# A fused attention and feed-forward kernel: all weight casts on VectorE, nine landing slots, eight float32 steps in the second product

## The chip, the cores and the metric

The kernel runs on one core of one Trainium2 chip. The metric is the device time of one execution in microseconds; the kernel before has a median of 746.74 us over three runs (746.36 to 748.03).

## The reference

Eight batches of 576 rows pass through an attention over 32 memory slots per head (8 heads of 64), and the result through a feed-forward block with weights of 512 x 2048 and 2048 x 512:

```python
a = softmax(phi over the 32 memory slots)             # per batch, head, row
k_m = einsum('bhsm,bhsd->bhmd', a, k)                 # 32 x 64 per head
v_m = einsum('bhsm,bhsd->bhmd', a, v)
attn = softmax((q @ k_m^T) / sqrt(64))                # 576 x 32 per head
x = concatenate over heads of (attn @ v_m)            # 4608 x 512
h = x @ w_in                                          # 4608 x 2048
g = h * erf(softplus(h))
out = g @ w_out                                       # 4608 x 512
```

## The kernel before, in words

**Tiling.** The work goes through 128 steps. A step is one batch b of 8 and one block k of 16, where a block is 128 of the 2048 hidden columns (`ORDER`, L273). The kernel never forms x: per batch it multiplies v_m into w_in on TensorE (`vw`, L624), and the *first product* (`ffn1`, L698, matmuls at L711) multiplies the attention weights by that, giving 128 hidden columns by 576 rows in two halves of 288. A copy out of PSUM gives h (L726, L727), ScalarE makes softplus and erf of it (L734, L739) in groups of steps (`GROUPS`, L274: four groups of 4, then groups of 6), since the two functions need different tables. `g_split` (L742) multiplies by h. The *second product* (`ffn2`, L799, matmuls at L795) adds g times w_out into four PSUM tiles of 128 rows; the last 64 rows of each batch (the "rest") go through DRAM (`rest_d`) and are taken for two batches together (`ffn2_rest`, L819).

**Two precisions of matmul.** Most products are made from values split in a rounded half and a remainder in the type fp32r: three matmuls (rounded by rounded, and the two mixed ones) stand for one. To split costs a ScalarE instruction (L362) and a VectorE one (L364) for weights and attention, and a VectorE cast (L765) and subtraction (L766) for g. The first steps work without a split, in plain float32, each matmul as two instructions: steps below `FR1` in the first product, steps below `FR2` in the second. `FR2` is 4. For these steps g is multiplied into its tile by L749 alone, and GpSimd splits only the rest's 64 columns (L759, L760), which SP then stores (L770). The block's chunk of w_out is used as decoded (`raw_of`) and is split later for the following batches: `split_wo` of chunk c is put at step `second[2c] - 2`, or, for a chunk that float32 steps use, at `second[16 + 2c] - 5`.

**The weights' way in.** Each of the 16 chunks (8 of w_in, called in0 to in7, and 8 of w_out, out0 to out7) is 1 MB. `load_weight` (L382) takes a slot of the pool `wo`, clears the slot's last 16-bit column with a memset on GpSimd (L385) and loads the rest by a DMA on SP (L387). The load lies one 16-bit piece off, and `decode` (L413) puts the numbers together again: a cast of the top pieces (on VectorE, L447, or on GpSimd, L448), a scaling of the low pieces (ScalarE, L449, or VectorE, L451), and a merge on VectorE (L442). A chunk of w_in is merged into a tile `wi`, which has two slots of two chunks each, and this tile is stored to DRAM (`w_in_d`, L457) for the later batches; its landing slot is then free. A chunk of w_out is merged in place.

**The slots.** The pool `wo` has `WB = NPR + 2`, that is 10, slots (NPR is 8). In this order it holds the first two tiles of q, the 16 chunks, and the split chunks of w_out (L465). A tile gets a slot only when every earlier one has one. So the split tiles come after all loads, and each split frees the slot of the chunk that it was made from.

**The order.** `Plan.order` (L125) is a list scheduler that runs when the kernel is built. Each operation has an engine or several ways (`other`), a cost in ns and a rank (100 times the step at which it is wanted). The scheduler keeps clocks for the engines and for landings, counts slots, takes for an operation with several ways the one that ends first (`best_way`, L150), and writes each engine's queue in the resulting order. On the chip every engine runs its queue in that order and waits where an input is late. The cast has the cost 1330 on VectorE and 2300 on GpSimd, a memset 100 on GpSimd, a load's issue 60 on SP. A memset and the load into the same tile wait for one another in the order in which the scheduler happened to write them.

Of the kernel before, what the change touches and what calls it, by code (L numbers as in the profile page):

```python
# [29 lines left out]
PE, DVE, ACT, POOL, SP = "PE", "DVE", "ACT", "POOL", "SP"  # L30
# [38 lines left out]
class Plan:  # L69
# [21 lines left out]
    def op(self, engine, cost, rank, reads, writes, emit, kind=None, nbytes=0, edge=None, after=(),  # L91
           holds=(), other=()):
        x = Op({engine: (cost, emit), **dict(other)}, rank, kind, nbytes, edge)
        x.before.update(after)
        for w, keys in ((False, reads), (True, writes)):
            for k in keys:
                k, part = (k[0], k[1]) if isinstance(k[0], tuple) else (k, None)
                x.tiles.add(k)
                for q, (wrote, read) in self.seen.setdefault(k, {}).items():
                    if q == part or q is None or part is None:  # L100
                        x.before.update(wrote)
                        if w:
                            x.before.update(read)
        for w, keys in ((False, reads), (True, writes)):
            for k in keys:
                k, part = (k[0], k[1]) if isinstance(k[0], tuple) else (k, None)
                s = self.seen[k]
                if w and part is None:
                    s.clear()
                wrote, read = s.setdefault(part, ([], []))  # L110
                if w:
                    wrote[:] = [x]
                    read.clear()
                else:
                    read.append(x)
        x.before.discard(x)
        for k in x.tiles:
            if k in self.users:
                self.users[k].append(x)
                x.placed.append(k)  # L120
        x.placed += [k for k in holds if k not in x.tiles]
        self.ops.append(x)
        return x
# [113 lines left out]
def tile_memory_attention_then_erf_softplus_ffn(  # L237
# [11 lines left out]
    nc = tc.nc  # L249
# [11 lines left out]
    NPR = DFF // 256  # L261
# [6 lines left out]
    assert NC == -(-S // ROW) and D < ROWS[-1]  # L268
    RAW = 5
    HB, EB, GB = 8, 7, 3  # L270
    WB = NPR + 2
    SCALE = 1.0 / float(D) ** 0.5
    ORDER = [(b, k) for b in range(B) for k in range(NK)]  # L273
    GROUPS = [4] * 4 + [6] * 18 + [2, 2]  # L274
    LAG = 8
    assert sum(GROUPS) == NS
    FR1, FR2 = 4, 4
    H_EITHER = 16

    pools = {  # L280
# [1 line left out]
        for n, b, kw in (  # L282
            ("const", 1, {}),
            ("wo", WB, {}),
            ("wi", 2, {}),
# [12 lines left out]
    const = pools["const"]  # L298
    room = {"wo": WB, "wi": 2, "vw_hi": 2, "vw_lo": 2, "at_hi": 4, "at_lo": 4, "h": HB, "e": EB}
    room.update({"g": GB, "rx": 2, "rr": 2, "raw": RAW, "ps": 4, "sc": 2, "dk": 1, "phiT": 2})  # L300
# [22 lines left out]
    def tile_(tag, *key, shape=None, dtype=F32, pool=None):  # L323
        key = plan.tile(tag, *key)
        p, s, d = SHAPES.get(tag, (pool, shape, dtype))
        T[key] = lambda: pools[p].tile(s, d, name=key[0], tag=tag, bufs=BUFS.get(tag))
        return key

    def get(key):
        if callable(T[key]):  # L330
            T[key] = T[key]()
        return T[key]
# [5 lines left out]
    def on_dve(n, inputs=2):  # L338
        return n / 0.96 + 85 if inputs == 2 else n / 1.92 + 75
# [73 lines left out]
    def decode(rank, name, c):  # L413
        key, n = ("w", name, c), 2 * DM
        dst = key
        if name == "in":
            w = ("wi", 0, c // 2)
            if c % 2 == 0:
                tile_("wi", *w)
            dst = (w, c % 2)  # L420

        def pieces():
            v = get(key).bitcast(U32).rearrange("p (n two) -> p n two", two=2)
            return v[:, :, 0], v[:, :, 1]

        def to():
            if name == "in":
                return get(w)[:, :, c % 2 * 256 : (c % 2 + 1) * 256]
            wf[c] = get(key).bitcast(F32)[:, :n].rearrange("p (j d) -> p j d", d=DM)
            return wf[c].rearrange("p j d -> p (j d)")  # L430

        def top(f):
            def emit():
                v = get(key).rearrange("p (n four) -> p n four", four=4)[:, :, 2]
                f(v.bitcast(F16), v.bitcast(BF16))
            return emit

        def merge():
            low, v = pieces()
            if name == "in":  # L440
                low, v = (x.rearrange("p (r f) -> p r f", r=NP_) for x in (low, v))
            nc.vector.scalar_tensor_tensor(  # L442
                out=to().bitcast(U32), in0=v, scalar=16, in1=low,
                op0=ALU.logical_shift_left, op1=ALU.bitwise_or)

        op(DVE, 1330, rank, [(key, "top")], [(key, "top")],
           top(lambda y, x: nc.vector.tensor_copy(out=y, in_=x)),  # L447
           other={POOL: (2300, top(lambda y, x: nc.gpsimd.tensor_copy(out=y, in_=x)))})  # L448
        op(ACT, 1330, rank, [(key, "low")], [(key, "low")], lambda: nc.scalar.activation(  # L449
            pieces()[0].bitcast(I32), pieces()[0], AF.Identity, scale=LOW),  # L450
           other={DVE: (on_dve(n, 1), lambda: nc.vector.tensor_scalar_mul(  # L451
               out=pieces()[0].bitcast(I32), in0=pieces()[0], scalar1=LOW))})
        op(DVE, on_dve(n), rank, [key], [dst], merge)
        if name == "out":
            raw_of[c] = dst
        elif c % 2:
            op(SP, 60, rank, [w], [("w_in", c // 2)], lambda: nc.sync.dma_start(  # L457
                out=w_in_d[c // 2], in_=get(w)), nbytes=P * 8192)
# [404 lines left out]
    for n, name in enumerate(FIRST):  # L863
        x, rank = int(name[-1]) if name[-1].isdigit() else 0, n - 2000
# [12 lines left out]

    memories(at(-10), at(-9), 0, EARLY)
    decode(at(-3), "in", 0)
    for u in range(2):  # L880
        attention(at(-8), at(-7 + 2 * u), u)
# [7 lines left out]
    for c in range(NPR):  # L889
        if c:  # L890
            when(2 * c - 3, decode, at(2 * c - 3), "in", c)
            when(2 * c - 1, vw, at(2 * c - 1.5), 0, c, 1, 2 * c < FR1)
        when(2 * c, decode, at(second[2 * c] - 2.5), "out", c)
        n = second[16 + 2 * c] - 5 if 2 * c < FR2 else second[2 * c] - 2
        when(n, split_wo, at(n), c)
# [105 lines left out]
```

## Time and profile before

| | us |
|---|---|
| median of three runs | 746.74 |
| the profiled execution | 746.22 |
| its span in the trace | 743.6 |
| PE (TensorE) busy | 711.6 |
| DVE (VectorE) busy | 516.7 |
| ACT (ScalarE) busy | 387.7 |
| POOL (GpSimd) busy | 44.2 |

Nine casts of chunks run on VectorE (13.7 us together) and seven on GpSimd (20.5 us). In a group's row, the first part names line, engine, operation and tiles, "x" the count; behind the bar stand the busy time, the mean ns of one, the idle time of the engine just before these instructions, and what ended it. In a timeline each row is a start, a length and an operation, with the idle time in front of it in brackets. PE is TensorE's matmuls and PEld its weight loads. The granted clock is the share of full speed that TensorE was given.

### The profile page before, as it was taken

To read this page: it belongs to the slowest core of one execution; us is meant where nothing else is said; L and a number is where in the kernel's file an instruction comes from. 1 tells how busy PE (TensorE), PEld (TensorE's weight loads), DVE (VectorE), ACT (ScalarE), POOL (GpSimd) and SP (SyncE) were. 2 spreads that over 40 slices of the span, in tenths; PEclk is the share of its full clock that TensorE was granted. 3 is DMA by queue.
4 is the path that set the end of the run, shared out by engine and by line. 5 is a ranking of instruction groups with operands and counts; after the bars stand their busy time and mean duration, and the time that the engine had idled before them with its cause. 6 is when DMAs were issued, how large, how long until landed. Compare 5 with 4: busy or idle time off the path is not lost.

```text
span 743.6 us, 12315 instructions
## 1 busy us (share of the span) xinstructions
PE 711.6 (96%) x4899; PEld 566.3 (76%) x4899; DVE 516.7 (69%) x956; ACT 387.7 (52%) x603; POOL 44.2 (6%) x69
## 2 busy tenths in 40 slices
PE   8866699999999999999999999999999999999997
PEld 3442377887888888888888878888888878888886
DVE  3664999989945597786963867687675567865730
ACT  3642677855942457366381638436454272653701
POOL 0014420000000000000000000000000000002230
PEclk9988799999999999999999999999999999999999
DMA  9996496556362353626262456335241343201002
GB/s 337 417 378 225 126 323 217 207 195 199 111 226 72 127 182 122 225 68 218 77 224 92 160 170 235 106 110 188 68 145 58 123 127 89 86 22 58 1 0 71
DMA packets 66666, 114.96 MB, mean 155 GB/s; under 512 B 37553, under 2 KB 45745, under 8 KB 62513
## 3 DMA queue, kind: packets, MB, share of 16 engines
q1 hardware_dynamic: 66608, 114.18, 45.0%
q8 instruction: 38, 0.62, 0.3%
q14 instruction: 20, 0.16, 0.1%
HBM read 93.19 MB, written 20.97 MB: 154 GB/s over the span
## 4 chain that ended last, share of the span: by engine, by line
PE 82%; DMA 12%; DVE 5%; issue 0%; ACT 0%; SPq 0%; POOL 0%; POOLq 0%; DVEq 0%; ACTq 0%
PE pso L795 44%; PE psh L711 24%; PE psr L795 6%; DMA w<-w_in 6%; PE psa L613 5%; DMA kv<-kv 3%; PE psa L561 2%; DMA phiT<-phiT 1%; DMA out<-ot 1%; DVE w L442 1%; DVE w L447 1%; DVE wi L442 1%; PE psa L583 0%; DVE pmx L477 0%; DVE e L749 0%
## 5 line engine op out<-in xcount | busy, mean ns | idle before, releaser
L795 PE MATMUL pso<-wo,g 128*128 128x512 f32 x1488 | 369.0, 394 | 0.5 <-DVE g L766 0.5
L795 PEld LDWEIGHTS pso<-wo,g 128*128 128x128 f32 x1488 | 270.7, 188 | 61.8 <-issue 9.7
L734 ACT ACTIVATE e<-h 128x576 f32<-128x576 f32 x128 | 86.1, 683 | 209.0 <-DVE h L726 208.5
L726 DVE COPY h<-psh 128x288 f32<-128x288 f32 x240 | 106.8, 451 | 27.6 <-PE psh L711 26.4
L765 DVE CAST g<-e 128x576 fp32r<-128x576 f32 x124 | 56.2, 454 | 86.1 <-PE pso L795 76.7
L711 PE MATMUL psh<-at_hi,vw_hi 128*128 128x288 f32 x496 | 111.2, 306 | 4.6 <-DVE vw_lo L364 4.5
L711 PEld LDWEIGHTS psh<-at_hi,vw_hi 128*128 128x128 f32 x496 | 85.8, 192 | 32.0 <-DVE vw_lo L364 6.5
L711 PE MATMUL psh<-at_lo,vw_hi 128*128 128x288 f32 x496 | 107.7, 299 | 0.0
L711 PE MATMUL psh<-at_hi,vw_lo 128*128 128x288 f32 x496 | 107.3, 298 | 0.0
L749 DVE TENSOR_TENSOR e<-e,h 128x576 f32<-128x576 f32 x124 | 90.8, 750 | 14.6 <-ACT e L739 14.6
L766 DVE TENSOR_TENSOR g<-e,g 128x576 fp32r<-128x576 f32 x124 | 93.2, 752 | 1.7
L711 PEld LDWEIGHTS psh<-at_hi,vw_lo 128*128 128x128 f32 x496 | 81.3, 192 | 0.0
L711 PEld LDWEIGHTS psh<-at_lo,vw_hi 128*128 128x128 f32 x496 | 80.7, 191 | 0.0
L739 ACT ACTIVATE e<-e 128x576 f32<-128x576 f32 x128 | 80.3, 676 | 0.3
L362 ACT ACTIVATE vw_hi<-psa 128x512 fp32r<-128x512 f32 (+1 forms) x68 | 35.2, 554 | 46.1 <-PE psa L613 45.9
L775 POOL CAST rr<-g 128x64 fp32r<-128x64 f32 x32 | 17.8, 566 | 610.0 <-DVE g L765 604.8
L364 DVE TENSOR_TENSOR vw_lo<-psa,vw_hi 128x512 fp32r<-128x512 f32 (+1 forms) x68 | 41.9, 634 | 11.8 <-ACT vw_hi L362 11.7
L795 PE MATMUL psr<-wo,rr 128*128 128x512 f32 x192 | 49.1, 392 | 0.0
L795 PEld LDWEIGHTS psr<-wo,rr 128*128 128x128 f32 x192 | 36.1, 188 | 7.9
L613 PE MATMUL psa<-wi,vm 64*32 64x512 f32 (+1 forms) x576 | 37.9, 566 | 3.9 <-DVE vw_lo L364 2.2
L842 ACT ACTIVATE ot<-pso 128x512 f32<-128x512 f32 x32 | 18.6, 592 | 41.6 <-PE pso L795 35.5
L734 ACT ACT_TABLE_LOAD x24 | 30.8, 1283 | 2.3 <-DVE h L726 1.9
(73 smaller groups left out, 499.4 us busy)
## 6 DMA issues: line engine op xcount, KB each, us to landing
wi<-w_in_d SPq DMA_DIRECT2D x28, 1024.0 KB, 5.3
kv<-kv SPq DMA_DIRECT2D x32, 640.0 KB, 8.2
q<-qT SPq DMA_DIRECT2D x16, 576.0 KB, 6.1
out<-ot SPq DMA_DIRECT2D x32, 256.0 KB, 2.1
w<-w_in SPq DMA_DIRECT2D x8, 1023.8 KB, 16.5
w<-w_out SPq DMA_DIRECT2D x8, 1023.8 KB, 11.6
rr<-rest_d SPq DMA_DIRECT2D x28, 256.0 KB, 2.9
rest_d<-g SPq DMA_DIRECT2D x108, 64.0 KB, 2.1
```

The lines of the kernel that those rows point to most:

```text
L362: lambda: nc.scalar.activation(get_hi(), get_src(), AF.Identity))
L364: lambda: nc.vector.tensor_tensor(out=get_lo(), in0=get_src(), in1=get_hi().bitcast(F32), op=ALU.subtract))
L613: nc.tensor.matmul(out=get(ps[par])[p * M : (p + 1) * M, :], lhsT=w()[rows, p, :], rhs=x()[rows, p, :], start=True, stop=True,)
L711: nc.tensor.matmul(out=get(ps), lhsT=x[:, g, k % 4 * P : (k % 4 + 1) * P], rhs=y[:, g, :], start=(n + g == 0), stop=(n == len(parts) - 1 a ...
L726: lambda: nc.vector.tensor_copy(out=keep(), in_=get(ps)),
L734: last[:] = [op(ACT, on_act(S), rank, [("h", i)], [e], lambda: nc.scalar.activation(get(e), get(("h", i)), AF.Softplus), kind="softplus", ...
L739: last[:] = [op(ACT, on_act(S), rank, [e], [e], lambda: nc.scalar.activation(get(e), get(e), AF.Erf), kind="erf", edge=edge, after=last)]
L749: op(DVE, on_dve(S), rank, [e, h], [to if i >= FR2 else (t, 0)], lambda: nc.vector.tensor_tensor(out=get(t)[:, 0].bitcast(F32) if i < FR2 ...
L765: op(DVE, on_dve(S, 1), rank, [e], [(t, 0)], lambda: nc.vector.tensor_copy(out=get(t)[:, 0], in_=get(e)))
L766: op(DVE, on_dve(S), rank, [e, (t, 0)], [(t, 1)], lambda: nc.vector.tensor_tensor(out=get(t)[:, 1], in0=get(e), in1=get(t)[:, 0].bitcast(F ...
L795: nc.tensor.matmul(out=o, lhsT=y, rhs=z, start=(start and n == 0), stop=(stop and n == len(parts) - 1))
L842: lambda: nc.scalar.activation(get(t)[:, :DM], get(o), AF.Identity))
```

## The change

Three things: the cast of a chunk's top pieces has only VectorE as its way; the pool `wo` has 9 slots instead of 10; and the second product uses float32 for steps 0 to 7 instead of 0 to 3. By the rule above the splits of chunks 2 and 3 of w_out thus move from steps 8 and 10 to steps 23 and 25.

```diff
-    WB = NPR + 2
+    WB = NPR + 1
...
-    FR1, FR2 = 4, 4
+    FR1, FR2 = 4, 8
...
         op(DVE, 1330, rank, [(key, "top")], [(key, "top")],
-           top(lambda y, x: nc.vector.tensor_copy(out=y, in_=x)),
-           other={POOL: (2300, top(lambda y, x: nc.gpsimd.tensor_copy(out=y, in_=x)))})
+           top(lambda y, x: nc.vector.tensor_copy(out=y, in_=x)))
```

## The prediction

> **What bounds the kernel now.** I read the page first, for where TensorE is not full.
>
> ```profile
> span 743.6 us, 12315 instructions
> PE   8866699999999999999999999999999999999997
> ```
>
> The profiled execution took 746.2 us: this span and 2.6 us around it. The median shown is 746.7, half a microsecond more. One digit is the busy tenths of 18.6 us. TensorE is short in the first five slices and full from the sixth on. So I split the span by hand, at the points where TensorE's filling changes (columns: length, busy us and instructions of PE, PEld, DVE, ACT and POOL, granted clock, DMA share, GB/s).
>
> ```profile
> 32.00:42.00 10.00, 5.14 (x20) 3.38 (x19) 2.26 (x4) 4.11 (x8) 2.79 (x7) 0.99 0.99 386
> 42.00:61.00 19.00, 17.21 (x80) 11.74 (x80) 9.86 (x18) 9.25 (x15) 0.00 (x0) 0.82 0.84 326
> 61.00:103.00 42.00, 26.93 (x196) 16.65 (x196) 36.98 (x44) 23.54 (x39) 22.63 (x19) 0.76 0.67 222
> 103.00:200.00 97.00, 96.47 (x735) 77.23 (x737) 90.07 (x171) 73.38 (x113) 0.00 (x0) 1.00 0.56 193
> ```
>
> From 103 to 200 us TensorE lacks 0.5 us of 97, and the page's row stays at 9 to the last slice. What it gets done earlier before 103 brings the end forward, and whatever matmul time is added makes the end later. Between 32 and 103 us it lacks 4.9 + 1.8 + 15.1 = 21.8 us, and at the granted clocks of 0.82 and 0.76 another 17.21 x 0.18 + 26.93 x 0.24 = 9.6 us: 31 us are the most that any change of this stretch could win. Next, the waits from 30 to 110 us (total, times, longest).
>
> ```profile
> PE pso L795 <- issue: 8.2, 2, 6.9
> PE psh L711 <- DVE vw_lo L364: 4.5, 1, 4.5
> PE psa L490 <- ACT bias L484: 4.3, 2, 3.9
> DVE w L442 <- POOL w L448: 18.3, 2, 10.5
> POOL w L385 <- DMA w<-w_in: 55.8, 5, 26.1
> ```
>
> VectorE waited twice, 18.3 us in all, at the merge of a chunk (L442) for its cast on GpSimd (L448). The timelines of GpSimd and VectorE say why (start, length, operation, and in brackets the idle time in front).
>
> ```profile
> 35.01 0.10 POOL L385 MEMSET w<- 128x1 uint16 x1 [2.41 <-DMA w<-w_out]
> 37.55 0.20 POOL L385 MEMSET w<- 128x1 uint16 x4 [2.44 <-DMA w<-w_in]
> 37.69 2.45 POOL L448 CAST w<-w 128x1024 f16<-128x1024 bf16 x1
> 61.05 0.14 POOL L385 MEMSET w<- 128x1 uint16 x2 [20.92 <-DMA w<-w_in]
> 61.13 4.72 POOL L448 CAST w<-w 128x1024 f16<-128x1024 bf16 x2
> 71.43 6.95 POOL L448 CAST w<-w 128x1024 f16<-128x1024 bf16 x2
> 91.35 2.89 POOL L448 CAST w<-w 128x1024 f16<-128x1024 bf16 x1 [0.63 <-DMA w<-w_out]
> 95.89 3.46 POOL L448 CAST w<-w 128x1024 f16<-128x1024 bf16 x1 [1.65 <-DMA w<-w_out]
> ...
> 40.17 1.23 DVE L442 SCALAR_TENSOR_TENSOR w<-w 128x1024 uint32<-128x1024 uint32 x1 [7.74 <-POOL w L448]
> 63.61 3.08 DVE L442 SCALAR_TENSOR_TENSOR w<-w 128x1024 uint32<-128x1024 uint32 x1 [10.51 <-POOL w L448]
> 72.85 3.21 DVE L447 CAST w<-w 128x1024 f16<-128x1024 bf16 x1
> 77.37 1.84 DVE L442 SCALAR_TENSOR_TENSOR w<-w 128x1024 uint32<-128x1024 uint32 x1
> 92.00 3.07 DVE L442 SCALAR_TENSOR_TENSOR w<-w 128x1024 uint32<-128x1024 uint32 x1
> 97.17 3.02 DVE L442 SCALAR_TENSOR_TENSOR wi<-w 128x1024 uint32<-128x1024 uint32 x1
> ```
>
> GpSimd runs its queue in order. Its casts stand behind one-column memsets (L385) that wait for a landing, until 37.5 and again for 20.9 us until 61.0. The chunks to be cast had landed before: the merges at 40.17 and 63.61 are of out0 and out1 (I place them by the order of the chunks), and out1's own memset is one of those released before 35. So the 7.7 and the 10.5 us are waits for a place in a queue, not for data. TensorE's 4.5 us wait (for a vw_lo, queued on VectorE behind the first merge) and its 6.9 us wait (second product of step 2, which reads out1) are their images.
>
> **Part by part: the casts.** Durations as least/median/greatest, and the groups of the operations that the longer float32 stretch drops and adds (busy us, mean ns):
>
> ```profile
> L448 POOL CAST w<-w x7: 2449/2894/3677, 37.7 to 95.9; 128x1024 f16<-128x1024 bf16 x7
> L447 DVE CAST w<-w x9: 1261/1314/3205, 14.5 to 95.7; 128x1024 f16<-128x1024 bf16 x9
> L765 DVE CAST g<-e 128x576 fp32r<-128x576 f32 x124 | 56.2, 454 | 86.1 <-PE pso L795 76.7 <-DMA rest_d<-g 7.9 <-POOL rr L775 1.0
> L766 DVE TENSOR_TENSOR g<-e,g 128x576 fp32r<-128x576 f32 x124 | 93.2, 752 | 1.7
> L364 DVE TENSOR_TENSOR wo<-w,wo 128x1024 fp32r<-128x1024 f32 x8 | 9.7, 1208 | 0.0
> L759 POOL CAST rx<-g 128x64 fp32r<-128x64 f32 x4 | 2.1, 526 | 0.0
> L760 POOL TENSOR_TENSOR rx<-g,rx 128x64 fp32r<-128x64 f32 x4 | 2.4, 599 | 0.3
> ```
>
> Seven casts move to VectorE: 7 x 1.31 = +9.2 us there. The five long VectorE rows above all lie beside a cast on GpSimd; against 1.23 for a merge and 1.31 for a cast they lose 1.85 + 1.90 + 0.61 + 1.84 + 1.79 = 8.0 us, which goes. With the seven casts gone, the two waits of 18.3 us go as such. What replaces them on VectorE is a cast that waits for its own landing, and behind it in VectorE's queue the copies of h (L726) and vw_lo, for which TensorE waits. For out0 and out1 this is nothing; for the later chunks it is the second rival.
>
> **Eight float32 steps.** Steps 4 to 7 lose their rounding (L765) and remainder (L766) on VectorE: 4 x (0.454 + 0.752) = -4.8 us. The splits of out2 and out3 (2 x 1.21 us on VectorE) leave the stretch for steps 23 and 25, where VectorE is 93% busy and TensorE full; I cost them there at nothing, 2.4 us at most if VectorE falls behind. On TensorE a step of the second product is eight float32 instructions instead of twelve:
>
> ```profile
> 57.33 3.60 PE L795 MATMUL pso<-w,g 128*128 128x512 f32 x8
> 67.83 6.01 PE L795 MATMUL pso<-w,g 128*128 128x512 f32 x8 [6.91 <-issue]
> 103.40 5.76 PE L795 MATMUL pso<-wo,g 128*128 128x512 f32 x24
> 43.10 0.68 PE L711 MATMUL psh<-at_lo,vw_hi 128*128 128x288 f32 x2
> 52.38 0.42 PE L711 MATMUL psh<-at_hi,vw_hi 128*128 128x288 f32 x2
> ```
>
> At full clock 3.60 against 5.76 / 2 = 2.88: 4 x 0.72 = +2.9 us. After a gap, at the lower clock, a float32 step took 6.01: up to 4 x (6.01 - 2.88) = +12.5. I take 2.9, since the stretch should be denser than now. GpSimd gets four more pairs of L759 and L760, 4 x 1.13 = 4.5 us, on an engine that loses seven casts.
>
> ```profile
> 87.61 1.40 POOL L759 CAST rx<-g 128x64 fp32r<-128x64 f32 x1
> 85.11 2.34 DVE L442 SCALAR_TENSOR_TENSOR wi<-w 128x1024 uint32<-128x1024 uint32 x2
> 87.63 1.29 DVE L447 CAST w<-w 128x1024 f16<-128x1024 bf16 x1
> ```
>
> At 87.6 it is GpSimd's instruction that becomes long (1.40 us), while VectorE's cast beside it keeps its 1.29; so I cost these pairs at nothing for VectorE, with 8 x 0.56 = 4.5 us as the other end, if all eight new ones block it.
> The Trainium skill speaks against this part: SBUF — State Buffer, section Who interferes with whom, says that a VectorE instruction with two SBUF inputs and a GpSimd instruction that reads SBUF exclude each other, and that the one to issue first holds the ports. The five long rows agree (3.08 us for 1.23), and by it the new pairs would cost VectorE up to those 4.5 us.
>
> **Nine slots.** Four of the opening loads, not five, get their memset behind them (the planner gives a memset 100 ns and a load 60). The tenth load, in4, now waits for the slot of the first queries, and its memset for the fourth landing, at 35.0; before, it had landed by 37.5. Its issue thus falls at about 35, with DMA at 0.99: it lands some 5 to 10 us later. I take its merge to be the first of the two at 85.11, so this is hidden by some 40 us, or 5 to 10 if the merges move up to 50. In7 must wait for in4's merge, out6 for in5's, out7 for in6's. Later memsets meet a GpSimd without casts, so the planner puts them ahead of their loads, and the long wait until 61.0 should not return.
>
> **The sum.** Directly on TensorE: 4.5 + 6.9 = 11.4 us of waits go. With them goes the low clock after each: a pair of the first product takes 0.68 us at 43 and 0.42 at 52, so the nine pairs of steps 4 and 5 that run before the next gap lose some 2 (the 0.26 holds a little of the pairs' overlap), and the step at 67.83 loses 6.01 - 3.60 = 2.4 more. Together 15.8. VectorE allows it: 18.3 + 8.0 - 9.2 + 4.8 + 2.4 = 24.3 us sooner at most. Off go 2.9 for float32, and I give back 3.1, by choice, for what is late next (the landing of the stored first-weight block, for which in4's merge waits, or the 4.3 us at L490, whose input is also on VectorE). That is -9.8: 746.2 - 9.8 = 736.4, and 736.9 beside the median; I say 736.7.
>
> **Rivals.** *More comes free.* The whole stretch moves up as far as VectorE allows: 24.3 - 2.9 = -21, 725. For it: VectorE is 88% busy from 61 to 103, so its release counts nearly in full. Against it: every wait would have to vanish.
> *Casts wait in VectorE's queue.* If the planner puts them ahead of their landings, the 18.3 us stay under another name. Then 8.0 + 4.8 + 2.4 - 9.2 = 6.0 us come free, half of it where TensorE waits: 3.0 less 2.9 is no change, 746.6. Against it: out0 and out1 are there.
> *The landing memsets still hold SP and GpSimd until 61.* Then only the 6.9 us wait goes, less 2.9: 742.7.
> *Slower: float32 at the lower clock.* If gaps stay in front of steps 4 to 7, they cost +12.5, and only 6.9 is won: +5.6, 752. It decides where a gap of about 4 us stands before each of them, as 6.91 stands before the row at 67.83. For it: the granted clock of 0.76. Against: float32 steps need no split, so TensorE has more to do while it waits.
> The Trainium skill, TensorE: Matmul & The Clock Gate, section What's actually happening, gives this mechanism: one idle window of some 3.4 us halves the clock. The 6.91 us gap followed by 6.01 for 3.60 agrees.
>
> **How the numbers follow.** Forecast 0.42, more comes free 0.18, memsets 0.14, casts wait 0.10, lower clock 0.16. About 0.2% (1.5 us) is what a measurement tells from no change. Faster: 0.42 + 0.18 + 0.14 and four of the ten hundredths of the fourth case, 0.78; same 0.06; slower 0.16. The range goes from 724 (the largest release) to 749: 746.6 and, above it, the 2.4 us of the moved splits; what is left out is the lower-clock case and little else. The forecast's own range is 730 to 742.
>
> **What would show it.** Right: no L448 rows; 16 casts on L447 at about 1.3 us, none of 3; no wait of L442 for POOL; matmuls of step 4 (first L711 of at_lo) starting near 35 instead of 43.10; 64 float32 L795 rows, most at full clock; TensorE full from about 90 instead of 103. Wrong: new VectorE waits on DMA at L447 of several us; L795 float32 rows of 6 us; SP waiting on L385 until 60.

## The result

The kernel after takes 716.0 us (median; 715.1 to 716.9), the kernel before 746.6 (median with one run more than above): a ratio of 0.959 (95% interval 0.957 to 0.961). 30.5 us came free where 9.8 were forecast, and the time lies below the range of 724 to 749. Run once more beside some of the experiments, it gave 715.0 and 0.960 (0.957 to 0.962).

TensorE's granted clock in the page of before (each digit 18.6 us):

```profile
PEclk9988799999999999999999999999999999999999
```

The page of the profile after:

```profile
span 714.4 us, 12285 instructions
PE   7999999999999999999999999999999999999997
PEclk9999999999999999999999999999999999999999
```

From the second slice on the dip is gone in TensorE's busy share, and its clock stays at 9 throughout. To see how much of the 29.2 us of span lies there, I look for the point at which TensorE has done the same work in both traces, and measure from there to the end. The windows of the kernel before:

```profile
0.00:103.00 103.00, 76.55 (x621) 45.05 (x621) 68.35 (x100) 52.74 (x91) 26.44 (x37) 0.87 0.82 304
103.00:743.60 640.60, 635.10 (x4281) 521.28 (x4279) 448.35 (x857) 334.91 (x513) 17.75 (x32) 1.00 0.39 131
```

And of the kernel after:

```profile
0.00:73.00 73.00, 66.16 (x613) 38.03 (x614) 58.36 (x92) 54.96 (x91) 7.05 (x29) 1.00 0.99 387
73.00:714.40 641.40, 636.36 (x4272) 519.28 (x4270) 451.46 (x859) 338.91 (x518) 22.59 (x41) 1.00 0.41 135
```

What filled 103 us before takes 73, and the rest is as long as it was (640.6 and 641.4 us, with nearly the same number of matmuls). The 30 us split in two: TensorE's idle time falls from 103 - 76.6 = 26.4 to 6.8 us (19.6), and its busy time from 76.6 to 66.2 (10.4), because a granted clock of 0.87 has become 1.00 (76.6 x 0.87 = 66.6). The same 71 us window as in the prediction, before and then after:

```profile
32.00:103.00 71.00, 49.27 (x296) 31.78 (x295) 49.09 (x64) 36.90 (x62) 25.42 (x26) 0.81 0.76 273
```

```profile
32.00:103.00 71.00, 68.21 (x485) 43.43 (x484) 67.76 (x106) 65.02 (x103) 11.10 (x27) 1.00 0.98 376
```

All engines but GpSimd are fuller: TensorE 49 to 68 us, VectorE 49 to 68, ScalarE 37 to 65, the DMA engines 0.76 to 0.98. VectorE's casts and the float32 steps in the kernel after (groups, then TensorE's and VectorE's timelines; the kernel after has a line fewer, so that the matmuls of L795 are at L794 and the scaling on ScalarE at L448):

```profile
L447 DVE CAST w<-w 128x1024 f16<-128x1024 bf16 x16 | 21.1, 1332 | 0.0
L442 DVE SCALAR_TENSOR_TENSOR w<-w 128x1024 uint32<-128x1024 uint32 x8 | 9.8, 1225 | 0.6 <-ACT w L448 0.6
L450 DVE TENSOR_SCALAR w<-w 128x1024 int32<-128x1024 uint32 x2 | 1.4, 716 | 0.0
...
37.31 0.42 PE L710 MATMUL psh<-at_lo,vw_hi 128*128 128x288 f32 x2
49.43 8.75 PE L794 MATMUL pso<-w,g 128*128 128x512 f32 x20
...
35.68 1.32 DVE L447 CAST w<-w 128x1024 f16<-128x1024 bf16 x1
```

No cast takes 3 us any more, no merge waits for GpSimd, the first pair of this kind starts at 37.3 us instead of 43.1 and at full clock, and twenty float32 matmuls in a row take 8.75 us. GpSimd's queue became in the main what I had said. Its memsets, and two of the loads that SP issues:

```profile
34.37 0.30 POOL L385 MEMSET w<- 128x1 uint16 x6 [1.26 <-DMA w<-w_out]
61.30 0.10 POOL L385 MEMSET w<- 128x1 uint16 x1 [13.90 <-issue]
85.08 0.10 POOL L385 MEMSET w<- 128x1 uint16 x1 [18.52 <-ACT e L738]
85.12 0.77 POOL L758 CAST rx<-g 128x64 fp32r<-128x64 f32 x1
...
61.43 0.33 SPq L387 DMA_DIRECT2D w<-w_in  x1
72.00 0.53 SPq L387 DMA_DIRECT2D w<-w_out  x1
```

The memset at 61.3 stands ahead of its load, which SP issues at 61.43; it waited for a slot. Only the one at 85.1 stands behind its load (issued at 72.00), though the row puts the 18.5 us down to ScalarE, and a float32 tail (L758) stands behind it in turn. Here nobody is late for it; the experiments show a kernel in which somebody is.

### The profile page after: what moved, and what is told of

Same layout as the page of the kernel before. It is cut to its first block, busy times and chain, and to the rows that moved or that the text cites. A ratio compares the mean times of both kernels' runs of the same rounds, so it can differ in the third digit from the quotient of the medians.

```text
span 714.4 us, 12285 instructions
## 1 busy us (share of the span) xinstructions
PE 702.5 (98%) x4883; PEld 557.3 (78%) x4883; DVE 509.8 (71%) x950; ACT 393.9 (55%) x608; POOL 29.6 (4%) x70
## 4 chain that ended last, share of the span: by engine, by line
PE 91%; DMA 3%; DVE 3%; ACT 2%; SPq 1%; issue 0%; ACTq 0%; DVEq 0%
PE pso L794 49%; PE psh L710 28%; PE psr L794 6%; PE psa L612 6%; PE psa L560 2%; DMA q<-qT 2%; DMA rest_d<-g 1%; ACT w L448 1%; DVE vw_lo L364 0%; SPq L401 0%; PE psa L582 0%; DVE w L447 0%; DVE h L725 0%; DVE at_lo L364 0%; PE psa L489 0%
## 5 line engine op out<-in xcount | busy, mean ns | idle before, releaser
L794 PE MATMUL pso<-wo,g 128*128 128x512 f32 x1440 | 356.4, 394 | 0.0
L794 PEld LDWEIGHTS pso<-wo,g 128*128 128x128 f32 x1440 | 262.1, 188 | 59.5 <-issue 7.4
L764 DVE CAST g<-e 128x576 fp32r<-128x576 f32 x120 | 54.3, 453 | 86.6 <-PE pso L794 76.5
L710 PE MATMUL psh<-at_lo,vw_hi 128*128 128x288 f32 x496 | 106.1, 295 | 0.0
L748 DVE TENSOR_TENSOR e<-e,h 128x576 f32<-128x576 f32 x120 | 87.7, 750 | 15.2 <-ACT e L738 15.2
L765 DVE TENSOR_TENSOR g<-e,g 128x576 fp32r<-128x576 f32 x120 | 90.2, 752 | 1.7
L710 PEld LDWEIGHTS psh<-at_hi,vw_lo 128*128 128x128 f32 x496 | 79.8, 188 | 0.6 <-DVE vw_lo L364 0.6
L710 PEld LDWEIGHTS psh<-at_lo,vw_hi 128*128 128x128 f32 x496 | 79.1, 188 | 0.0
L794 PE MATMUL psr<-wo,rr 128*128 128x512 f32 x192 | 49.1, 392 | 0.0
L794 PEld LDWEIGHTS psr<-wo,rr 128*128 128x128 f32 x192 | 36.1, 188 | 7.9
L841 ACT ACTIVATE ot<-pso 128x512 f32<-128x512 f32 x32 | 18.6, 591 | 40.7 <-PE pso L794 33.8
L794 PE MATMUL pso<-w,g 128*128 128x512 f32 x64 | 29.8, 600 | 1.8 <-DVE g L748 1.8
```

Source lines behind the costliest of these rows:

```text
L710: nc.tensor.matmul(out=get(ps), lhsT=x[:, g, k % 4 * P : (k % 4 + 1) * P], rhs=y[:, g, :], start=(n + g == 0), stop=(n == len(parts) - 1 a ...
L748: op(DVE, on_dve(S), rank, [e, h], [to if i >= FR2 else (t, 0)], lambda: nc.vector.tensor_tensor(out=get(t)[:, 0].bitcast(F32) if i < FR2 ...
L764: op(DVE, on_dve(S, 1), rank, [e], [(t, 0)], lambda: nc.vector.tensor_copy(out=get(t)[:, 0], in_=get(e)))
L765: op(DVE, on_dve(S), rank, [e, (t, 0)], [(t, 1)], lambda: nc.vector.tensor_tensor(out=get(t)[:, 1], in0=get(e), in1=get(t)[:, 0].bitcast(F ...
L794: nc.tensor.matmul(out=o, lhsT=y, rhs=z, start=(start and n == 0), stop=(stop and n == len(parts) - 1))
L841: lambda: nc.scalar.activation(get(t)[:, :DM], get(o), AF.Identity))
```

## The experiments

Theory A: the harm was done in GpSimd's queue, in which casts stand behind memsets that wait for a landing. Theory B: the float32 steps 4 to 7, which need no split weights, fill TensorE. Theory C: the casts on GpSimd are harmful by themselves, being long and colliding with VectorE. Ratios are to the kernel before on the same chip.

**The parts one by one.** Only the casts (before, without L448's way):

```diff
-           top(lambda y, x: nc.vector.tensor_copy(out=y, in_=x)),
-           other={POOL: (2300, top(lambda y, x: nc.gpsimd.tensor_copy(out=y, in_=x)))})
+           top(lambda y, x: nc.vector.tensor_copy(out=y, in_=x)))
```

> The kernel before with one edit: the cast has only VectorE as its way; ten slots and four float32 steps stay. Theory A (GpSimd's queue, in which casts stood behind memsets that wait for landings, is the whole cause): 716 to 721 us, TensorE idle in 32-103 us down from 21.8 to under 6. Theory B (TensorE is filled by the float32 steps 4 to 7, which need no split): about half of the gain, 728 to 735, with new TensorE waits near the first fp32r step of the second product. If the slots or the float32 steps were needed to unlock it: above 740.

719.6 us, 0.965 (0.962 to 0.968): 3.5 of the 4.1% come from this edit alone. The time is Theory A's forecast (C says the same here); TensorE's idle time from 32 to 103 us is 6.5 us, a little over the "under 6", at a clock of 1.00. B is out as the main cause.

Only the float32 steps (before, with `FR1, FR2 = 4, 8`):

> The kernel before with one edit: eight float32 steps in the second product; casts stay on both engines and ten slots stay. Theory A: the two waits of VectorE for GpSimd stay (18 us), so within 4 us of before, or slower by up to 12.5 us if steps 4 to 7 run at the lower clock: 743 to 759. Theory B: 728 to 735.

743.7 us, 0.997 (0.995 to 1.000). The large waits of the kernel before are there; this is VectorE's row from 30 to 110 us:

```profile
DVE w L442 <- POOL w L448: 18.4, 2, 11.5
```

The kernel after with four float32 steps again, `FR1, FR2 = 4, 4`:

> The kernel after with one edit undone: four float32 steps instead of eight; nine slots, all casts on VectorE. Theory A: float32 costs 2.7 us of TensorE time, so 713 to 718, the same or slightly faster than after, unless VectorE (4.8 us more in a stretch where it is 95% busy) holds TensorE up: then up to 724. Theory B: 725 or more.

722.1 us, 0.969 (0.965 to 0.972): about 1% slower than the kernel after, though TensorE has less to do, and within the wider bound (724) that A gave for a late VectorE. By the order of the slots a split can start only when every load has had one (here the last load is issued at 76.82 and the first split begins at 79.53), and TensorE waits for the first splits (by their order, those of out2):

```profile
80.63 0.49 PE L794 MATMUL pso<-wo,g 128*128 128x512 f32 x1 [1.45 <-ACT wo L362]
81.97 0.73 PE L794 MATMUL pso<-wo,g 128*128 128x512 f32 x2 [0.85 <-DVE wo L364]
```

These two waits are 2.3 us of the 6; the granted clock from 32 to 103 us is 0.95 besides.

The kernel after with ten slots, `WB = NPR + 2`:

> The kernel after with one edit undone: ten landing slots instead of nine. All theories: slots are worth little once GpSimd's queue is free, 714 to 718 us. The fifth opening memset waits again for its own landing, 2.5 us later (37.5 instead of 35); if SP's loads behind it matter, some 2 us slower than after; if the tenth slot's earlier load matters, up to 2 us faster.

717.6 us, 0.963 (0.960 to 0.966): the slots are worth nothing that is clear of the intervals, as forecast. Between four and eight float32 steps there is with ten slots hardly a difference (0.965 and 0.963).

The kernel after with the casts' way over GpSimd given back:

> The kernel after with the casts' way over GpSimd given back: nine slots and eight float32 steps, casts on either engine. Theory A: the waits behind the memsets return, 738 to 755. If nine slots and float32 steps carry the gain: 716 to 725.

753.8 us, 1.011 (1.008 to 1.014). The same nine slots and float32 steps that go with 716 us are slower than before when five casts stay on GpSimd. In its waits and on GpSimd:

```profile
PE pso L795 <- issue: 15.3, 1, 15.3
DVE g L749 <- POOL rx L760: 13.2, 1, 13.2
...
52.26 0.14 POOL L385 MEMSET w<- 128x1 uint16 x2 [16.84 <-DMA w<-w_out]
52.34 4.74 POOL L448 CAST w<-w 128x1024 f16<-128x1024 bf16 x2
103.31 0.10 POOL L385 MEMSET w<- 128x1 uint16 x1 [19.88 <-DMA w<-w_out]
103.36 0.32 POOL L760 TENSOR_TENSOR rx<-g,rx 128x64 fp32r<-128x64 f32 x1
```

Casts and now float32 tails too stand behind landings.

**The queue order alone.** One edit makes the planner write a memset ahead of its load, so that it waits only for its slot:

```diff
-        load(rank, P * 8190, [(key, "top"), (key, "low")],
+        load(rank, P * 8190, [(key, "top"), (key, "low"), (key, "end")],
```

In the kernel before, all seven casts staying on GpSimd:

> The kernel before with one edit: the planner must write a slot's memset ahead of the load into it, so that no memset on GpSimd waits for a landing; the seven or so casts stay on GpSimd, ten slots, four float32 steps. Theory A (the queue order is the cause): most of the gain comes without moving a cast, 718 to 728 us, and the merges no longer wait for GpSimd by more than 3 us at a time. Theory C (the casts themselves are the cause: 2.4 to 3.7 us each on GpSimd, and VectorE's instructions beside them at 3 instead of 1.2 us): 735 to 745.

732.6 us, 0.981 (0.977 to 0.984): some 13 to 14 of the 30 us come back with no cast moved. (The edit changes what the planner works with, so other places in the queues move too. The profiled execution was the fastest, 728.1.) It lies between A's forecast and C's; I take it that both have a part. From 30 us on no merge of VectorE waits for GpSimd any more, but the casts are as long as before, and some still collide with VectorE:

```profile
30.72 5.18 POOL L448 CAST w<-w 128x1024 f16<-128x1024 bf16 x2
50.94 5.94 POOL L448 CAST w<-w 128x1024 f16<-128x1024 bf16 x2
33.50 3.23 DVE L442 SCALAR_TENSOR_TENSOR w<-w 128x1024 uint32<-128x1024 uint32 x1
```

The same edit in the last kernel of the list above (nine slots, eight float32 steps, casts on either engine):

> Nine slots, eight float32 steps, casts on either engine, and every memset ahead of its load. Without that order it took 753.8. Theory A: the waits for landings go and the price of the casts themselves stays, as in the kernel before with memsets first (732.6): 722 to 735. If casts on GpSimd do the harm by themselves: 745 or more.

725.5 us, 0.974 (0.972 to 0.976). 753.8 fell to 725.5: there the order was worth 28 us, as A said. What still separates this kernel from the kernel after, 9 to 10 us, goes with the five casts on GpSimd, by whatever way. The same edit in the kernel after:

> The kernel after with the same edit: every memset ahead of its load. Theory A: what GpSimd's queue still cost the kernel after is the SP stop until 34.5 us (a memset behind the fourth landing) and float32 tails behind a memset at 61 to 85 us; TensorE is idle for only 2.8 us in 32-103, so 713.5 to 716.5. If loads wait longer for their memsets now, up to 718.

715.5 us, 0.959 (0.957 to 0.961): no difference, as forecast. With ten slots:

> The kernel after with ten slots and every memset ahead of its load. With ten slots alone it took 717.6, and with memsets first alone 715.5. If the fifth opening memset behind its landing is what ten slots cost: 713 to 716. If it is the planner's other order: 716 to 719.

718.1 us, 0.964 (0.961 to 0.966): as with ten slots alone, so the fifth memset is not what ten slots cost. The unchanged kernel after took 715.0 on the same chip and no two executions overlap: ten slots with this order are about 3 us (0.4%) slower. That it is the planner's other order was only the forecast's guess.

**Casts that nobody waits for.** The kernel after with memsets first, and eight casts of a spare tile added on GpSimd:

```diff
+        clear = op(POOL, 100, rank, [], [(key, "end")], ...)
+        if c >= 4:
+            op(POOL, 2300, rank, [], [("spare",)], lambda: nc.gpsimd.tensor_copy(
+                out=spare_top().bitcast(F16), in_=spare_top().bitcast(BF16)), after=(clear,))
```

> The kernel after with every memset ahead of its load (as in the run of that edit alone, 715.5 us) and eight extra casts of a spare tile on GpSimd, one behind the memset of each of the last eight chunks; nobody waits for their result. What they can cost is VectorE's time beside them (the five long rows of the profile before lost 8.0 us to seven casts) and loads or float32 tails that stand behind them in GpSimd's queue. If the collision of the two engines is a main part of the gain: 721 to 727, with VectorE instructions of about 3 us. If casts on GpSimd cost only because results are waited for: 714 to 718.

729.3 us, 0.979 (0.977 to 0.982): 14 us slower than without them. That is more than I had allowed for. VectorE's long rows (its cast, L447, is at L456 here), a GpSimd cast and a TensorE wait beside them, and SP's wait for memsets from 20 to 110 us:

```profile
29.55 3.24 DVE L456 CAST w<-w 128x1024 f16<-128x1024 bf16 x1
46.37 2.75 DVE L456 CAST w<-w 128x1024 f16<-128x1024 bf16 x1
70.47 3.34 DVE L456 CAST w<-w 128x1024 f16<-128x1024 bf16 x1
...
29.12 2.51 POOL L393 CAST spare<-spare 128x1024 f16<-128x1024 bf16 x1
49.69 2.08 PE L803 MATMUL pso<-w,g 128*128 128x512 f32 x2 [3.14 <-DVE g L757]
...
SPq L396 <- POOL w L391: 20.8, 3, 11.3
```

The last row in the run without the spare casts:

```profile
SPq L387 <- POOL w L385: 6.3, 2, 6.1
```

Both things are there. All sixteen casts on VectorE take 30.3 us instead of the 20.9 of the run without spare casts, and SP waits 14.5 us longer for memsets. What reaches TensorE is mostly VectorE: of its 11.3 us of gaps from 20 to 103 us (2.8 without spare casts) 9.6 are put down to VectorE, the longest of them right behind the stretched cast at 46.37, and none to a landing; VectorE's own waits in that time name no landing either. The granted clock of 0.94 adds about 4 us. So the collision looks to be the larger part; an exact division of the 14 us this run does not give. The Trainium skill, SBUF — State Buffer, section Who interferes with whom, says that where VectorE and GpSimd contend, the instruction that issues second waits for the whole of the first. The first long row agrees: the GpSimd cast beside it ends at 31.63, and VectorE's cast, begun at 29.55, ends at 32.79. By that page an instruction with one input contends only in some of VectorE's modes, and no run here shows the mode of the cast.

**Number of float32 steps.** The kernel after with twelve:

> The kernel after with twelve float32 steps instead of eight. Theory A: the stretch is full on TensorE, so four more float32 steps cost 4 x 0.68 = 2.7 us: 717 to 720. Theory B (float32 steps relieve a short VectorE): the same or faster, 712 to 716.

720.1 us, 0.965 (0.963 to 0.967): 4.1 us slower than the kernel after, where A had 2.7 and at most 720. With six:

> The kernel after with six float32 steps. Four steps gave 722.1, eight 716.0, twelve 720.1. If float32 steps serve to bridge until the first split weights are there, six is between four and eight: 716 to 720. If the cost of 0.68 us a step on TensorE decides: 713 to 716.

732.6 us, 0.983 (0.980 to 0.986), far from every forecast. The chain is plain: out7's load is issued at 74.36, a memset that was written behind it waits for its landing, a float32 tail stands behind the memset, VectorE waits for the tail and TensorE for a copy on VectorE (GpSimd, VectorE and TensorE):

```profile
86.67 0.10 POOL L385 MEMSET w<- 128x1 uint16 x1 [22.78 <-DMA w<-w_out]
86.73 0.32 POOL L759 TENSOR_TENSOR rx<-g,rx 128x64 fp32r<-128x64 f32 x1
...
87.08 0.46 DVE L764 CAST g<-e 128x576 fp32r<-128x576 f32 x1 [16.25 <-POOL rx L759]
...
87.97 0.85 PE L710 MATMUL psh<-at_hi,vw_hi 128*128 128x288 f32 x2 [13.59 <-DVE h L725]
```

So memsets go first there too:

> The kernel after with six float32 steps, and every memset ahead of its load. Six steps alone took 732.6, with VectorE idle for 16.3 us behind a float32 tail on GpSimd that stood behind a memset waiting 22.8 us for the landing of its own load. If the landing memset is the cause of that, the 17 us come back: 713 to 718. If six float32 steps are themselves a bad number for the stretch: 728 or more.

717.2 us, 0.962 (0.960 to 0.964). 15 of the 17 us came back: the number six was not the fault. And with four steps and memsets first:

> The kernel after with four float32 steps, and every memset ahead of its load. Four steps alone took 722.1. If float32 steps themselves hardly matter and landing memsets made the difference of 6 us: 714 to 717. If the float32 steps 4 to 7 are what bridges the wait for the first split weights: 720 to 724.

724.1 us, 0.972 (0.969 to 0.975), no better than four steps alone. Here the landing memsets are not the cause; with nine slots float32 steps 4 to 7 are worth 6 to 9 us, whatever they bridge. In this run TensorE waits once for 4.6 us,

```profile
PE psa L612 <- ACT h L726: 4.6, 1, 4.6
```

where the run without the edit waited for splits. What gates it in the one and the other I have not settled further.

The unchanged kernel after, as a mark for the runs with spare casts, six steps, and ten slots with memsets first:

> The kernel after, unchanged, as the mark for the others on this chip: 714 to 717 by all theories.

715.0 us, as forecast. No version is clearly faster than it.

## Why the prediction was wrong, and where it was right

*Right: where the time lay, and why.* The stretch from 32 to 103 us was named as the only one with anything to win, 31 us at most, and 30 came from it. The cause, chunks that had landed but whose casts stood in GpSimd's queue behind another chunk's landing, is shown for about half of it: the order alone gave 13 to 14 us in one kernel and 28 in another. Another 10 us or so go only when the casts leave GpSimd.

*Wrong: the sum.* The step that failed is its first: "Directly on TensorE: 4.5 + 6.9 = 11.4 us of waits go", with 4.4 us of low clock. I added up the waits that name the casts and left the others, some 10 us of idle time and 5 of low clock, as if they were causes of their own. They were consequences: with the casts off GpSimd, the 4.3 us at L490 (its input sat on a VectorE that was late), the waits for vw_lo and h, and the low clock after every gap went as well; the run with that edit alone has 6.5 us of idle time left of 21.8, a clock of 1.00 and no wait of TensorE at this place. The result is 19.6 us of idle time and 10.4 of clock, nearly the whole of the bound.

*Wrong: the 3.1 us given back "by choice".* Nothing was late next. TensorE's waits from 30 to 103 us are now 2.8 us in two groups:

```profile
PE pso L794 <- DVE g L748: 1.8, 1, 1.8
PE psh L710 <- DVE vw_lo L364: 1.0, 2, 0.7
```

*Too low: VectorE's bound of 24.3 us*, and with it the first rival (725) and the range's lower end. From the start to the points of equal work on TensorE (103 and 73 us, the windows above) VectorE's idle time falls by 20.0 us, where 18.3 were counted, and its busy time by 10.0, where 6.0 were. Over the whole span its busy time falls by only 6.9, so about 3 us were put off beyond 73: the bound asked VectorE to have made up everything by one point in time. It also did not see that the planner, with its choices open, would give three of VectorE's five scalings of low pieces to ScalarE (two L450 are left): 3 x 0.7 us.

*Right: the casts and the collisions.* 9.2 us were put on VectorE and 8.0 taken off: the sixteen casts take 1.33 us each, and none is stretched. The float32 steps at full clock: twenty matmuls in 8.75 us are 3.5 us a step against the 3.6 assumed. Four more such steps, the run with twelve, cost 4.1 us, where 2.9 were counted for four. The added pairs on GpSimd cost VectorE nothing that shows: the merges' mean is 1.23, what a merge took before without a collision. So the 4.5 us by the rule of the Trainium skill, SBUF — State Buffer, section Who interferes with whom, were no price here.

*Right but for one: the slots and the later memsets.* Nine slots cost nothing, and in4's load is issued at 34.53 us, as forecast (about 35). That "the planner puts them ahead of their loads" holds for eight of the nine later memsets; the wait until 61.3 is one for a slot. Out7's memset, at 85.1 us, stands behind its load. That this is harmless is luck of the order; with six float32 steps the same memset's wait cost 15 us.

*The slower rival* did not occur: TensorE has one gap of 1.8 us before the first matmuls of the second product and none before steps 4 to 7, and the granted clock is 1.00. A chain like it is seen in the run with the casts given back to GpSimd, 753.8 us, with a TensorE wait of 15.3 us before a second product and a granted clock of 0.85 from 32 to 103 us.

## What to carry to other kernels

In a queue that is worked in order, look at what the cheapest instruction waits for: a memset of 0.1 us behind a landing held back casts, tails and loads, and cost up to 28 us. When the engine that sets the end is idle in a stretch and every wait there leads back to one late queue, price the fix with all of the stretch's idle time and low clock, down to the next bound, and not with the waits that name the queue: here the first gave 31 us, the second 15.8, and 30.5 were measured. An edit to such an order can turn the sign of another edit: eight float32 steps and nine slots were 1% slower with casts on GpSimd and part of a 4% gain without them.

## What was not expected of the hardware

Eight casts on GpSimd whose result nobody uses cost 14 us, about 1.7 us each, where a VectorE cast takes 1.3 us in all. With them VectorE's own sixteen casts take 9.4 us more, four of them, beside a GpSimd cast, 2.8 to 3.3 us each instead of 1.3.
